# Gated linear attention with an ELU feed-forward on one core: w_in products of 512 columns over pairs of blocks

## The chip, the cores and the metric

The kernel runs on one core of a Trainium2 chip. The metric is the device time of one execution in microseconds (us). Matrix products run on TensorE (PE in the profile, its weight loads PEld), the rest on VectorE (DVE), ScalarE (ACT) and GpSimd (POOL); SyncE (SP) issues nearly all DMAs.

## The reference

```python
def _attn_ref(q, k, v, alpha):            # (B, H, S, D) = (4, 8, 768, 48)
    state = zeros((B, H, D, D))
    for t in range(S):
        state = alpha[:, :, t, :, None] * state + einsum('bhd,bhe->bhde', k[:, :, t], v[:, :, t])
        y[:, :, t] = einsum('bhd,bhde->bhe', q[:, :, t], state)
    return y

def _moe_ref(x, w_in, w_out):             # x: 3072 tokens x 384, w_in 384 x 2048, w_out 2048 x 384
    h = x @ w_in
    g = where(h > 0, h, exp(minimum(h, 0)) - 1)
    return g @ w_out                      # x is y with the heads side by side
```

All tensors are float32. The weights reach the kernel as 64-bit words.

## The kernel before

The attention runs in 24 windows of 128 tokens (`W`; 6 windows per batch element), each cut into two chunks of 64, for all 8 heads at once. The feed-forward runs in 12 blocks of 256 tokens (`BLK`), two windows each, and 8 pairs of 128 hidden columns a block (`NJ`). Each step is a small function, named in an order written out by hand: `START` for the first four blocks, where the weights are unpacked too, and `STEADY`, one round for each later block, with numbers relative to the round. Each engine works through its own instructions in this order.

A window i goes through: L or LA, LB and LV (loads of k, q, alpha and of v), SC (running products of alpha, VectorE), LN and EX (ScalarE), KA, KB, KC (scaled k; VectorE or POOL by the lists KAV, KBV), PC (a check sum), SQ (scaled q), TP and KN or TA, TB, T (k transposed by TensorE and copied by ScalarE, or by VectorE in blocks of 32), S (scores, TensorE), MK (mask), U (new state, TensorE), UA, UB, UC (state of the next window, VectorE), Y (outputs, TensorE), XH and XL (the outputs as two float32r parts, hi by ScalarE and lo by VectorE, in the tile xt), and XD (a DMA that moves the fourth pair of heads into the spare rows of xt). YL, Y3 and XP belong to the first windows.

A weight tile f is loaded by F, unpacked by DA, DB, DC (VectorE), split into two float32r parts by WH (ScalarE) and WL (VectorE, POOL or, after WP, ScalarE). LC, CA and CB read the weights again for a check. X is a filler: two warm-up matmuls of 512 columns without a use.

A step of the feed-forward (b, j) is: A (18 products h = x w_in: two tiles of 128 hidden columns, three tiles of x, three products of hi and lo parts each), RA and RB (ScalarE: relu and exp of -h), RC (VectorE: the ELU), GH and GL (the hi and lo parts of g), and O (12 products, summed over all j in two tiles o of 128 tokens). Z copies the two sums and stores them. V and VP evaluate the checks near the end.

All PSUM tiles (h, o, y, q, u, sc, tp and so on) come from one pool of eight buffers of 128 x 512 (`psa`, tag "pa"); r, gh and gl have three buffers each. Products, with 256 columns in A and 384 in O:

Of the kernel before, what the change touches and what calls it, by code (L numbers as in the profile page):

```python
# [8 lines left out]
F32 = mybir.dt.float32  # L9
# [7 lines left out]
W = 128  # L17
# [5 lines left out]
BLK = 256  # L23
# [6 lines left out]

EARLY = 6
# [17 lines left out]
X.2.2 LA.0 SC.0 LN.0 LB.0 EX.0 KA.0 KB.0 LA.1 SC.1 KC.0 LN.1 LB.1 EX.1 SQ.1 KA.1 KB.1 TP.0 SQ.0 KC.1 S.0 PC.0 MK.0  # L49
F.2 LV.0 KN.0 U.0 UC.0 TP.1 F.0 UA.0 S.1 LV.1 LV.3 KN.1 DA.0 DB.0 U.1 UP.1 UA.1 MK.1 YL.0 Y3.0 X.2.0 PC.1 DC.0 L.2  # L50
UC.1 L.3 YL.1 SC.2 WH.0 LN.2 Y.0 SQ.2 Y3.1 XH.0 EX.2 WH.2 WP.0 F.6 Y.1 SC.3 WL.0 KA.2 KB.2 F.4 KC.2 WP.2 TP.2 XH.1
LN.3 PC.2 XP.1 KN.2 DA.2 XP.0 DB.2 XL.0 XL.1 DC.2 S.2 WL.2 EX.3 WH.6 LV.2 U.2 WH.4 UA.2 KA.3 MK.2 F.1 A.0.0 RA.0.0
# [918 lines left out]
```

## Time and profile before

| | |
|---|---|
| median of 3 runs | 476.09 us (476.07 to 477.59) |
| the profiled execution | 475.45 us, span 473.7 us |
| granted TensorE clock | 0.999 |
| PE, DVE, ACT, POOL busy | 98%, 80%, 64%, 27% of the span |
| h products (L650) | 1728, 128x256 |
| o products (L703) | 1152, 128x384 |

The span goes from the first to the last instruction of the core; the execution's own time holds what lies around it. PE counts matmuls as busy from start to modelled end, and those overlap: what one product costs is read from the distance of starts, or from the pieces of the chain of waits, not from its mean length. In that chain each row is a piece of time: its start, its length, engine, tile and line, and how many instructions.

### The profile page before, as it was taken

To read this page: it belongs to the slowest core of one execution; us is meant where nothing else is said; L and a number is where in the kernel's file an instruction comes from. 1 tells how busy PE (TensorE), PEld (TensorE's weight loads), DVE (VectorE), ACT (ScalarE), POOL (GpSimd) and SP (SyncE) were. 2 spreads that over 40 slices of the span, in tenths; PEclk is the share of its full clock that TensorE was granted. 3 is DMA by queue.
4 is the path that set the end of the run, shared out by engine and by line. 5 is a ranking of instruction groups with operands and counts; after the bars stand their busy time and mean duration, and the time that the engine had idled before them with its cause. 6 is when DMAs were issued, how large, how long until landed. Compare 5 with 4: busy or idle time off the path is not lost.

```text
span 473.7 us, 13243 instructions
## 1 busy us (share of the span) xinstructions
PE 466.6 (98%) x5438; PEld 449.3 (95%) x5438; DVE 381.1 (80%) x770; ACT 303.9 (64%) x696; POOL 126.3 (27%) x111
## 2 busy tenths in 40 slices
PE   7999999999999999999999999999999999999996
PEld 3889999999999999999999999999999999999996
DVE  6999999789888978798898898798898898335331
ACT  4576668664664676867766866867766866655452
POOL 3021432535573512412412421422421520000000
PEclk9999999999999999999999999999999999999999
DMA  8999321621436035425424524424424231210011
GB/s 303 414 413 410 133 71 30 220 65 65 118 108 199 3 82 177 162 69 166 150 70 152 164 72 152 160 75 154 151 85 151 75 94 54 66 43 10 2 36 38
DMA packets 20483, 61.14 MB, mean 129 GB/s; under 512 B 2880, under 2 KB 7872, under 8 KB 20416
## 3 DMA queue, kind: packets, MB, share of 16 engines
q1 hardware_dynamic: 20128, 59.83, 37.9%
q8 instruction: 45, 0.74, 0.7%
q10 hardware_dynamic: 288, 0.39, 0.2%
q14 instruction: 22, 0.18, 0.1%
HBM read 53.53 MB, written 4.72 MB: 123 GB/s over the span
## 4 chain that ended last, share of the span: by engine, by line
PE 96%; ACT 1%; DVE 1%; DMA 1%; POOL 0%; issue 0%; POOLq 0%; DVEq 0%
PE h L650 41%; PE o L703 40%; PE y L452 4%; PE q L368 2%; PE y L447 2%; PE q L323 2%; PE wd L623 1%; PE sc L339 1%; PE tp L274 1%; PE y L492 1%; DMA qka<-in_qka_dram 1%; PE u L386 1%; DVE P L201 1%; PE yl L447 0%; ACT R L215 0%; PE wd L511 0%
## 5 line engine op out<-in xcount | busy, mean ns | idle before, releaser
L650 PE MATMUL h<-xt,w 128*128 128x256 f32 x1728 | 201.1, 276 | 0.2 <-DVE r L669 0.2
L650 PEld LDWEIGHTS h<-xt,w 128*128 128x128 f32 x1728 | 196.8, 192 | 1.5 <-PE tp L274 0.4
L703 PE MATMUL o<-w,gh 128*128 128x384 f32 x768 | 188.2, 327 | 0.0
L703 PEld LDWEIGHTS o<-w,gh 128*128 128x128 f32 x768 | 132.9, 189 | 0.5
L703 PE MATMUL o<-w,gl 128*128 128x384 f32 x384 | 125.3, 326 | 0.0
L658 ACT ACTIVATE r<-h 128x512 f32<-128x512 f32 x96 | 56.3, 597 | 64.3 <-PE h L650 57.2
L284 DVE STREAM_TRANSPOSE kn<-qka 32x128 f32<-32x128 f32 x256 | 77.4, 303 | 4.0
L669 DVE SCALAR_TENSOR_TENSOR h<-r,h 128x512 f32<-128x512 f32 x79 | 53.5, 690 | 28.2 <-ACT r L663 27.8
L703 PEld LDWEIGHTS o<-w,gl 128*128 128x128 f32 x384 | 72.6, 189 | 0.1
L689 DVE TENSOR_TENSOR gl<-h,gh 128x512 fp32r<-128x512 f32 x79 | 53.9, 689 | 18.6 <-ACT gh L675 16.3
L675 ACT CAST gh<-h 128x512 fp32r<-128x512 f32 x79 | 45.9, 581 | 35.6 <-DVE h L669 19.6
L663 ACT ACTIVATE r<-r 128x512 f32<-128x512 f32 x96 | 60.6, 635 | 1.9
L223 POOL TENSOR_TENSOR qka<-qka,R 128x512 f32<-128x512 f32 x18 | 23.2, 1286 | 138.5 <-ACT R L215 86.5
L253 POOL TENSOR_TENSOR st<-qka,P 64x512 f32<-64x512 f32 x30 | 38.0, 1268 | 23.0 <-DVE P L201 13.5
L351 DVE TENSOR_TENSOR st<-q,mask 64x256 f32<-64x256 f32 x72 | 30.3, 421 | 7.8 <-PE q L323 6.4
L228 POOL TENSOR_TENSOR R<-P,R 128x512 f32<-128x512 f32 x20 | 24.4, 1220 | 33.9 <-DVE qka L223 32.5
L210 ACT ACTIVATE R<-P 128x512 f32<-128x512 f32 x24 | 15.2, 631 | 26.9 <-DVE P L201 26.9
L689 POOL TENSOR_TENSOR gl<-r,gh 128x512 fp32r<-128x512 f32 x17 | 24.1, 1426 | 25.9 <-ACT gh L675 17.4
L201 DVE TENSOR_TENSOR_SCAN P<-qka,first 128x516 f32<-128x516 f32 x24 | 29.4, 1224 | 0.9 <-DMA qka<-in_qka_dram 0.8
L606 ACT ACTIVATE ck<-ck,lim 128x384 f32<-128x384 f32 x32 | 23.1, 721 | 0.7
L601 ACT ACTIVATE ck<-ck 128x384 f32<-128x384 f32 x32 | 21.5, 672 | 3.0 <-DMA ck<-in_wgt_dram 3.0
L233 DVE SCALAR_TENSOR_TENSOR qka<-R,qka 128x512 f32<-128x512 f32 x24 | 19.2, 800 | 1.8 <-POOL R L228 1.3
(105 smaller groups left out, 449.0 us busy)
## 6 DMA issues: line engine op xcount, KB each, us to landing
qka<-in_qka_dram SPq DMA_DIRECT2D x22, 770.0 KB, 5.3
raw<-in_wgt_dram SPq DMA_DIRECT2D x16, 768.0 KB, 13.7
ck<-in_wgt_dram SPq DMA_DIRECT2D x32, 384.0 KB, 3.3
vs<-in_vv_dram SPq DMA_DIRECT2D x36, 192.0 KB, 4.2
out_dram<-ot SPq DMA_DIRECT2D x22, 192.0 KB, 2.0
vs<-in_vv_dram SPq DMA_DIRECT2D x6, 384.0 KB, 9.7
xt<-y SPq DMA_DIRECT2D x40, 48.0 KB, 2.2
qka<-in_qka_dram SPq DMA_DIRECT2D x2, 512.0 KB, 5.0
```

Of the source, the lines that this page charges most:

```text
L201: nc.vector.tensor_tensor_scan(out=P.rearrange("p n w -> p (n w)"), data0=t[:, 2 * NP * W:], data1=first.rearrange("p n w -> p (n w)"), in ...
L228: eng(KBV, i).tensor_tensor(out=d["R"], in0=pw(i), in1=d["R"], op=ALU.mult)
L253: eng(SQV, i).tensor_tensor(out=st[r, a], in0=d["q"][r], in1=pw(i)[r], op=ALU.mult)
L284: nc.vector.transpose(out=kn[32 * t:32 * t + 32, :, 32 * g:32 * g + 32], in_=d["kt"][32 * g:32 * g + 32, :, 32 * t:32 * t + 32])
L351: nc.vector.tensor_tensor(out=d["st"][r, a, :, c * C:(c + 1) * C], in0=d["s4"][a][o], in1=mask[o].unsqueeze(1).broadcast_to([64, NP, C]), ...
L650: nc.tensor.matmul(h[:, f, :], lhsT=t[:, wi, ws], rhs=x[:, :, c, xi].rearrange("p a x -> p x a"), start=(f == 0 and k == 0), stop=(k == 8) ...
L658: nc.scalar.activation(out=r, in_=d["h"], func=AF.Relu, scale=-1.0)
L663: nc.scalar.activation(out=d["r"], in_=d["r"], func=AF.Exp, scale=-1.0)
L669: nc.vector.scalar_tensor_tensor(out=d["g"], in0=d["r"], scalar=-1.0, in1=d["h"], op0=ALU.add, op1=ALU.max)
L675: nc.scalar.copy(out=gh, in_=d["g"])
L689: q.tensor_tensor(out=gl, in0=d["g"], in1=d["gh"].bitcast(F32), op=ALU.subtract)
L703: nc.tensor.matmul(o[:, 0:DM], lhsT=gt[:, f, ms], rhs=t[:, wi, f * DM:f * DM + DM].rearrange("p (a x) -> p x a", a=2), start=(j == 0 and f ...
```

## The change

From block 4 on (`PB`) two blocks b and b + 1 are one pair of 512 tokens. The xt tile holds four windows. A step A of a pair computes one tile of 128 hidden columns for all 512 tokens, 9 products of 512 columns; b and j together number the 16 tiles of hidden columns. O takes one tile of hidden columns for four tiles of 128 tokens, so a pair has four sums o, held from its first step O to its last. Z acts once a pair and copies two of its sums by ScalarE and two by VectorE. The stores of the last pair (four, before two of the last block) are issued by ScalarE. START and STEADY, and the lists of who does what, are new. Two more windows go through Y in START. The scratch of dynamic DMAs shrinks to 2048 bytes.

```diff
+PB = 4
-WLV, KAV, KBV, SQV = (1, 7, 9, 10, 11, 14, 15), (0, 1, 2, 3, 4, 7), (0, 1, 2, 6), (1, 2, 3, 5, 7, 10, 11)
-WPE, XPE, GPE, UPE = (0, 2, 4, 6), (0, 1, 2), (), (1,)
+WLV, KAV, KBV, SQV = (1, 3, 9, 11, 13), (0, 1, 2, 3, 5, 6, 11), (0, 2, 3, 4, 5, 11), (0, 1, 5, 7, 9, 10, 11)
+WPE, XPE, GPE, UPE = (0, 2, 4, 6), (0, 1), (), (1,)
...
 STEADY = """
-Y.1 XH.1 Y.0 XL.1 A.-1 RA.-1 A.-3 RA.-3 RB.-3 A.-2 RC.-3 XH.0 XL.0 GH.-3 O.-5 GL.-3 ZV.4 V.0 RB.-1 RC.-1 CA.-12
+U.2 S.2 L.5 A.-3 MK.2.0 UA.2 UB.2 MK.2.1 UC.2 V.0 PC.3 SC.4 CA.-12 CB.-12 O.-5 U.3 S.3 RA.-3 LN.4 L.6 LC.-11 UA.3
...
     def xs(i):
-        blk, half = divmod(i, 2)
-        if blk not in xt:
-            xt[blk] = xpool.tile([128, 2, NC, 2, W], F32R, name="xt", tag="xt")
-        return xt[blk][:, half]
+        pr, k = divmod(i, 4)
+        if pr not in xt:
+            xt[pr] = xpool.tile([128, 4, NC, 2, W], F32R, name="xt", tag="xt")
+        return xt[pr][:, k]
...
     def A(b, j):
-        x = xt[b]
         h = psa.tile([128, 2, BLK], F32, name="h", tag="pa")
         ff[b, j] = dict(h=h)
-        for f in range(2):
+        x = xt[b // 2]
+        for f in range(2 if b < PB else 1):
             k = 0
-            t = wgts[2 * j]
+            r = 2 * j + f if b < PB else b % 2 * NJ + j
+            t = wgts[r // 2 * 2]
             for c in range(NC):
-                ws = slice(f * DM + c * 128, f * DM + c * 128 + 128)
+                ws = slice(r % 2 * DM + c * 128, r % 2 * DM + c * 128 + 128)
                 for wi, xi in ((0, 0), (0, 1), (1, 0)):
-                    nc.tensor.matmul(h[:, f, :], lhsT=t[:, wi, ws], rhs=x[:, :, c, xi].rearrange("p a x -> p x a"),
+                    if b < PB:
+                        o, xv = h[:, f, :], x[:, b % 2 * 2:b % 2 * 2 + 2, :, xi].rearrange("p a c x -> p c x a")[:, c]
+                    else:
+                        o = h.rearrange("p q x -> p (q x)")
+                        xv = x[:, :, c, xi].rearrange("p (q a) x -> p q x a", a=2)
+                    nc.tensor.matmul(o, lhsT=t[:, wi, ws], rhs=xv,
                                      start=(f == 0 and k == 0), stop=(k == 8), skip_group_check=True)
...
     def O(b, j):
-        if j == 0:
-            ops_[b] = [psa.tile([128, 512], F32, name="o", tag="pa") for _ in range(2)]
+        pair = b >= PB
+        key = b // 2 * 2 if pair else b
+        r0 = b % 2 * NJ + j if pair else 2 * j
+        nf = 1 if pair else 2
+        if r0 == 0:
+            ops_[key] = [psa.tile([128, 512], F32, name="o", tag="pa") for _ in range(4 if pair else 2)]
...
     def Z(b):
-        for m in range(2):
-            ot = gpool.tile([128, DM], F32, name="ot", tag="ot")
-            nc.scalar.copy(out=ot, in_=ops_[b][m][:, 0:DM])
+        if b >= PB and b % 2 == 0:
+            return
+        b0 = b // 2 * 2 if b >= PB else b
+        for m, o in enumerate(ops_.pop(b0)):
+            ot = gpool.tile([128, DM], F32, name="ot", tag="ot", bufs=4)
+            if m % 2 and b >= PB:
+                nc.vector.tensor_copy(out=ot, in_=o[:, 0:DM])
+            else:
+                nc.scalar.copy(out=ot, in_=o[:, 0:DM])
 
             q = nc.sync if b < NBLK - 1 else nc.scalar
-            q.dma_start(out=out[b * BLK + m * 128:b * BLK + m * 128 + 128, :], in_=ot)
-        del ops_[b], xt[b]
+            q.dma_start(out=out[b0 * BLK + m * 128:b0 * BLK + m * 128 + 128, :], in_=ot)
```

What stands in a row on TensorE in one round of the steady part. First before: the two Y (L452) stand together ahead of three steps A, and U and S (L368, L323, tile q) of both windows stand together, after one step O. U has half its products (x8) in the last window of a batch element.

```order
L703 MATMUL o<-w_851,gl 128x384
L452 MATMUL y<-st,vs_119 64x64 x16
L452 MATMUL y<-st,vs_118 64x64 x16
L650 MATMUL h<-xt,w_1138 128x256 x18
L650 MATMUL h<-xt,w_861 128x256 x18
```
```order
L703 MATMUL o<-w_851,gl 128x384
L368 MATMUL q<-vs_120,kn 48x48 x16
L323 MATMUL q<-st,qka_133 64x64 x16
L368 MATMUL q<-vs_121,kn 48x48 x8
L323 MATMUL q<-st,qka_134 64x64 x16
L703 MATMUL o<-w_1086,gh 128x384 x2
```

Now (L371 and L326 are U and S, L455 is Y, L659 A, L716 O): U and S of one window, a step A and a step O, U, S and Y, a step O (its first rows shown), and then the other Y ahead of two steps A.

```order
L371 MATMUL q<-vs_118,kn 48x48 x16
L326 MATMUL q<-st,qka_134 64x64 x16
L659 MATMUL h<-xt,w_392 128x512 x9
L716 MATMUL o<-w_714,gh 128x384 x2
L716 MATMUL o<-w_714,gl 128x384
```
```order
L371 MATMUL q<-vs_119,kn 48x48 x16
L326 MATMUL q<-st,qka_132 64x64 x16
L455 MATMUL y<-st,vs_118 64x64 x16
L716 MATMUL o<-w_668,gh 128x384 x2
L716 MATMUL o<-w_668,gl 128x384
```
```order
L716 MATMUL o<-w_668,gl 128x384
L455 MATMUL y<-st,vs_119 64x64 x16
L659 MATMUL h<-xt,w_392 128x512 x18
L716 MATMUL o<-w_668,gh 128x384 x2
L716 MATMUL o<-w_668,gl 128x384
```

Two clumps of small matmuls a round became three, and every step A has half the products, twice as wide.

TensorE's start, first before (L126 warm-ups and fillers, L274 TP, L339 S, L386 U, L412 UP, L447 YL and Y) and then now, where each line number is 3 higher:

```order
L126 MATMUL xf<-first 128x512
L274 MATMUL tp<-ident,qka_132 128x128 x4
L339 MATMUL sc<-st,qka_132 64x64 x16
L386 MATMUL u<-vs_118,kn 64x48 x16
L274 MATMUL tp<-ident,qka_133 128x128 x4
L339 MATMUL sc<-st,qka_133 64x64 x16
L386 MATMUL u<-vs_119,kn 64x48 x16
L412 MATMUL u<-vs_119,minus 128x192 x2
L447 MATMUL yl<-st,vs_118 64x64 x6
```
```order
L129 MATMUL xf<-first 128x512
L277 MATMUL tp<-ident,qka_132 128x128 x4
L342 MATMUL sc<-st,qka_132 64x64 x16
L389 MATMUL u<-vs_118,kn 64x48 x16
L129 LDWEIGHTS first
L129 MATMUL xf<-first 128x512
L129 LDWEIGHTS first
L129 MATMUL xf<-first 128x512
L450 MATMUL yl<-st,vs_118 64x64 x6
L277 MATMUL tp<-ident,qka_133 128x128 x4
L495 MATMUL y<-y_225,sel 64x128 x6
L450 MATMUL y<-st,vs_118 48x64 x18
```

The chain of window 0 goes through to its Y ahead of U and S of window 1, and fillers stand in between.

ScalarE's last instructions, before and now (L658 and L667 RA, L663 and L672 RB, L675 and L684 GH, L712 and L730 the copy in Z, L715 and L733 the store):

```order
L658 ACTIVATE r<-h 128x512
L663 ACTIVATE r<-r 128x512
L675 CAST gh<-h 128x512 x2
L712 COPY ot<-o 128x384
L715 DMA out_dram<-ot 128x384
```
```order
L667 ACTIVATE r<-h 128x512
L672 ACTIVATE r<-r 128x512
L684 CAST gh<-h 128x512 x2
L730 COPY ot<-o 128x384
L733 DMA out_dram<-ot 128x384 x2
```

In both, the copy and the stores come once more behind these rows. There are four stores now, two of them of copies by VectorE.

More of the change, by code (lines that the diff above doesn't have):

```diff
@@ new lines @@
+Y.2 MK.3.1 EX.4 MK.3.0 XH.2 O.-4 RB.-3 Y.3 XH.3 XL.2 A.-2 RC.-3 UB.3 GH.-3 RA.-2 RB.-2 XD.2 CA.-11 XL.3 GL.-3 UC.3
+KA.4 KB.4 SC.5 A.-1 LN.5 EX.5 O.-3 ZV.4 RA.-1 RB.-1 XD.3 KA.5 KB.5 LV.4 RC.-2 GH.-2 CB.-11 A.2 KC.4 T.4.0 T.4.3
+RC.-1 GL.-2 KC.5 A.0 LC.-10 RA.2 GH.-1 GL.-1 LC.-9 T.5.3 T.5.0 RA.0 RB.0 RC.0 T.5.2 CA.-10 CB.-10 RB.2 RC.2 GH.0
+GL.0 O.-2 O.-1 Z.-1 A.1 RA.1 RB.1 RC.1 GH.1 A.3 RA.3 CA.-9 RB.3 T.4.2 GL.1 SQ.5 RC.3 CB.-9 A.4 T.4.1 SQ.4 RA.4 GH.2
+GL.2 RB.4 RC.4 GH.3 GL.3 T.5.1 GH.4 O.0 O.1 O.2 GL.4 LC.-8 VP.0 PC.4 LV.5
@@ L694, in O @@
         gh, gl = d["gh"], d["gl"]
-        if j == 0:
-            ops_[b] = [psa.tile([128, 512], F32, name="o", tag="pa") for _ in range(2)]
-        for m in range(2):
-            o = ops_[b][m]
-            ms = slice(m * 128, m * 128 + 128)
-            for f in range(2):
-                t = wgts[2 * j + 1]
+        pair = b >= PB
[4 more added lines that the diff above has]
+            ops_[key] = [psa.tile([128, 512], F32, name="o", tag="pa") for _ in range(4 if pair else 2)]
+        for m, o in enumerate(ops_[key]):
+            for f in range(nf):
+                r = r0 + f
+                t = wgts[r // 2 * 2 + 1]
+                at = f * BLK + m * 128
                 for k, (gt, wi) in enumerate(((gh, 0), (gh, 1), (gl, 0))):
-                    nc.tensor.matmul(o[:, 0:DM], lhsT=gt[:, f, ms],
-                                     rhs=t[:, wi, f * DM:f * DM + DM].rearrange("p (a x) -> p x a", a=2),
-                                     start=(j == 0 and f == 0 and k == 0),
-                                     stop=(j == NJ - 1 and f == 1 and k == 2))
+                    nc.tensor.matmul(o[:, 0:DM], lhsT=gt.rearrange("p q x -> p (q x)")[:, at:at + 128],
+                                     rhs=t[:, wi, r % 2 * DM:r % 2 * DM + DM].rearrange("p (a x) -> p x a", a=2),
+                                     start=(r == 0 and k == 0), stop=(r == 2 * NJ - 1 and k == 2))
     @tok
     def Z(b):
-        for m in range(2):
-            ot = gpool.tile([128, DM], F32, name="ot", tag="ot")
-            nc.scalar.copy(out=ot, in_=ops_[b][m][:, 0:DM])
+        if b >= PB and b % 2 == 0:
[7 more added lines that the diff above has]
+                nc.scalar.copy(out=ot, in_=o[:, 0:DM])
             q = nc.sync if b < NBLK - 1 else nc.scalar
-            q.dma_start(out=out[b * BLK + m * 128:b * BLK + m * 128 + 128, :], in_=ot)
-        del ops_[b], xt[b]
+            q.dma_start(out=out[b0 * BLK + m * 128:b0 * BLK + m * 128 + 128, :], in_=ot)
     flag = []
@@ L957 @@
     wgt = np.ascontiguousarray(np.stack([wi, wo], axis=1)).view(np.int64).reshape(2 * NJ, 128, 2 * DM)
-    nc = bacc.Bacc("TRN2", target_bir_lowering=False, num_devices=1)
+    nc = bacc.Bacc("TRN2", target_bir_lowering=False, num_devices=1, dynamic_dma_scratch_size=2048)
     arrays, args = {}, []
```

62 lines of the change are left out of this document (29 added, 33 removed).

## The prediction

> **What bounds the kernel now.** I read the page first (busy shares, then the shares of the chain), then TensorE's waits, then the chain of waits over one block of the steady part, then the busy time of the same stretch.
>
> ```profile
> span 473.7 us, 13243 instructions
> PE 466.6 (98%) x5438; PEld 449.3 (95%) x5438; DVE 381.1 (80%) x770; ACT 303.9 (64%) x696; POOL 126.3 (27%) x111
> PE 96%; ACT 1%; DVE 1%; DMA 1%; POOL 0%; issue 0%; POOLq 0%; DVEq 0%
> ```
> TensorE's row of the waits (total, times, longest):
>
> ```profile
> PE wp L126 <- DVE first L120: 2.1, 1, 2.1
> PE tp L274 <- issue: 0.5, 1, 0.5
> PE h L650 <- DVE r L669: 0.2, 1, 0.2
> PE u L386 <- ACT kn L304: 0.2, 1, 0.2
> ```
> These four waits are all that TensorE has in the whole span: three at the start and a single one of 0.2 us later. Between the start and the last w_out product its stream has no hole, so every microsecond that TensorE's own instructions save or cost reaches the end, and other engines count only where they open a hole that isn't there now.
>
> The chain over one block (start, length, what):
>
> ```profile
> 232.26 7.80 PE o L703 x48
> 240.06 2.02 PE y L452 x64
> 242.08 6.22 PE h L650 x54
> 248.30 1.95 PE o L703 x12
> 250.25 0.51 PE q L368 x32
> 250.76 0.48 PE q L323 x32
> 251.24 0.36 PE q L368 x32
> 251.60 0.49 PE q L323 x32
> 252.09 4.10 PE o L703 x24
> 256.18 8.04 PE h L650 x72
> 264.22 1.95 PE o L703 x12
> ```
> And that stretch's busy time, in the order PE, weight loads, DVE, ACT, POOL:
>
> ```profile
> 232.30:268.20 35.90, 35.90 (x434) 35.31 (x433) 31.91 (x76) 24.91 (x61) 9.40 (x8) 1.00 0.42 128
> ```
> This is one block: 8 steps A and 8 steps O, and the attention of two windows in two clumps of small matmuls. A step A (18 products of 256 columns) takes 2.01 us, 111.7 ns a product (8.04 us for 72, four steps). A step O (12 of 384) takes 1.95 us, 162.5 ns each (7.80/48). The clumps also cost at their edges. After one, 54 products take 6.22 us instead of 54 x 111.7 = 6.03, and 24 w_out products 4.10 instead of 3.90: 0.20 us at the exit. At the entry the first U takes 0.51 us, the second, which follows small matmuls, 0.36: 0.15 us. So a clump costs 0.35 us beyond its work. VectorE is busy 31.91 of 35.90 us (89%), so it has 4 us a block to spare, in pieces.
>
> **The change, part by part.**
>
> *Long products.* From block 4 on a step A is 9 products of 512 columns. The trace has 512-column products only in the warm-up and fillers; from the timeline (start, length, count):
>
> ```profile
> 5.56 3.40 PE L126 MATMUL wp<-first 128*128 128x512 bf16 x15
> 8.80 0.38 PE L126 MATMUL xf<-first 128*128 128x512 bf16 x1
> 9.94 0.63 PE L274 MATMUL tp<-ident,qka 128*128 128x128 f32 x4 [0.55 <-issue]
> 11.82 1.27 PE L386 MATMUL u<-vs,kn 128*64 128x48 f32 x32 [0.17 <-ACT kn L304]
> ```
> Fifteen start between 5.56 and 8.80: 216 ns each. In proportion to the 384-column product it would be 216.7. The 256-column product lies 3.4 ns above that proportion (111.7 against 108.3); a long one that did so too would take 220. Bounds 216 and 220; I take 216, the row of this width. A step A is then 9 x 0.216 = 1.944 us, 0.066 less; 64 such steps (blocks 4 to 11) give -4.22 us (with 220: 9 x 0.220 = 1.98, -1.92).
>
> The Trainium skill ("TensorE: Matmul & The Clock Gate", section "Back-to-back issue gap") has a sustained 131 ns for a product of 512 columns in a stream of loads and products. The row above has 216 and 384 columns already take 162.5, so the trace disagrees; by that figure the 576 long products would take 75 us rather than 124.
>
> *More clumps.* Four more pieces of the chain, from the first four blocks (start, length, what):
>
> ```profile
> 17.34 0.54 PE xf L126 x2
> 45.87 0.20 PE y L511
> 81.55 0.44 PE tp L274 x4
> 81.98 1.95 PE o L703 x12
> ```
> The order of the changed kernel splits the attention of two windows into three clumps a block instead of two: U S, then U S Y, then the other Y, with a step O or A between. From the first w_in product to the end I count 25 clumps in the order before and 33 in the order now. Those of tp alone are left out: behind a lone tp the 12 products take their plain 1.95 us (the last two rows). 8 x 0.35 = +2.80 us. Bounds: the entry alone (8 x 0.15 = 1.2) and 0.20 at both edges (3.2). I take the rows' value.
>
> *First four blocks.* One more window is transposed by TensorE (TP, KN) instead of VectorE: +0.44. XP of window 2 goes: -0.20 on TensorE; VectorE does XL instead (0.55 by the row of L533 below) and loses the transposes of the one window, which are more. The filler X has five calls instead of two. Two of the five (four products) stand ahead of the first transposes, where TensorE now waits: the warm-ups end at 8.80 + 4 x 0.216 = 9.66, against 9.94, and the 0.17 us wait for kn ahead of the first U goes too, since SC of window 1 and SQ of window 0 are issued so that S comes first ready: -0.45. The other three calls stand where one stood: 2 x 0.54 = +1.08 (bounds 0, if TensorE would wait there anyway, and 1.08). VectorE's chain to the first weights (DA, DB, DC) keeps its length; on the SP queue the loads of alpha, k, q and v change places, but the same bytes stand ahead of the first weight pair. So I give both nothing; should the start hang on them, the gain of 0.45 goes.
>
> *The end.* The last A steps are now 6 and 7, and O 5, 6, 7 stand behind them; before, a step 6 had O 3 to 5 as cover.
>
> The groups of ScalarE and VectorE in the block shown above (count, busy, mean ns):
>
> ```profile
> L663 ACT ACTIVATE r<-r 128x512 f32<-128x512 f32 x8 | 5.1, 634 | 0.2
> L658 ACT ACTIVATE r<-h 128x512 f32<-128x512 f32 x8 | 4.7, 596 | 4.2 <-PE h L650 4.2
> L675 ACT CAST gh<-h 128x512 fp32r<-128x512 f32 x8 | 4.6, 578 | 2.2 <-DVE h L669 1.1 <-PE o L703 1.0
> L507 ACT ACTIVATE xt<-y 128x384 fp32r<-128x384 f32 x2 | 1.0, 490 | 0.0
> L506 ACT ACTIVATE y<-y 128x128 fp32r<-128x128 f32 x2 | 0.6, 276 | 0.0
> ```
> ```profile
> L669 DVE SCALAR_TENSOR_TENSOR h<-r,h 128x512 f32<-128x512 f32 x8 | 5.5, 690 | 1.5 <-ACT r L663 1.5
> L689 DVE TENSOR_TENSOR gl<-h,gh 128x512 fp32r<-128x512 f32 x8 | 5.4, 688 | 0.4 <-ACT gh L675 0.3
> L533 DVE TENSOR_TENSOR xt<-y,xt 128x384 fp32r<-128x384 f32 x2 | 1.1, 548 | 0.0
> ```
> The transfer of the last rows of xt (page, part 6), the chain's last piece on TensorE, and ScalarE's timeline at the end:
>
> ```profile
> xt<-y SPq DMA_DIRECT2D x40, 48.0 KB, 2.2
> ```
> ```profile
> 459.88 9.77 PE o L703 x60
> ```
> ```profile
> 468.69 0.48 ACT L712 COPY ot<-o 128x384 f32<-128x384 f32 x1 [4.45 <-PE o L703]
> 469.68 0.48 ACT L712 COPY ot<-o 128x384 f32<-128x384 f32 x1 [0.51 <-PE o L703]
> 470.19 0.34 ACTq L715 DMA_DIRECT2D out_dram<-ot  x1
> ```
> With A 6 ending at 0: ScalarE runs RA, RB of step 6 (to 1.25), waits for A 7 (1.94), runs RA, RB of 7 (to 3.2), then GH 6 (3.8); VectorE does RC 7 to 3.9 and only then GL 6, to 4.6. O 5 fills 1.94 to 3.89, and the third product of O 6 (4.2) waits for GL 6: +0.4 us, 0.5 with hand-overs. GL 7 is done at 5.3, ahead of O 7. Before, the last five O run without a hole (9.77 = 60 x 0.163). Then four sums are stored instead of two, by ScalarE's queue: copy, store, the store of a VectorE copy, copy, store, store. The third and fourth of them begin when the last sum is ready and need 0.48 + 2 x 0.34 = 1.16, where one copy and one store (0.82) stood: +0.4 with the wait for VectorE's copies. Together +0.9 (0.3, the stores alone, to 1.0).
>
> *At no cost, with the cover named.* Z comes once a pair; its two VectorE copies (near 0.55, the row of L533, which also reads 128x384 of such a buffer) stand where O 7 has ended and three steps A (5.8 us) follow before the next pair's first O. The first A of a pair needs the second Y of its own block's round, by way of XH (0.28 and 0.49, with a read of the accumulator between), XL (0.55) and XD on the SP queue: 1.6 us with hand-overs, and 2.2 for the transfer: two steps A and one O, 5.8 us, stand between. If VectorE were 2 us late there, that cover would be gone. POOL keeps KA, KB and SQ of the later windows, 9.40 of 35.90 us. Larger xt tiles and the smaller DMA scratch move no instruction. The w_out products keep their number and width.
>
> Sum: -4.22 + 2.80 + 0.44 - 0.20 - 0.45 + 1.08 + 0.9 = +0.35 us. The profiled execution took 475.45 us (span 473.7 and 1.75 around it); it would be 475.8. The median of the three runs, 476.09, stands 0.64 above that execution, so I add the sum to the median: 476.4. About 0.3%, 1.4 us, is what a measurement of this kernel can tell from no change.
>
> **The rivals.**
>
> *Faster.* The edges cost less than counted or fillers only fill. With half of the exit price hidden by the 216 ns that a long product gives the next load, 14 of the clumps now (two a block, seven blocks) lose 0.10 each of their exit, -1.4, and fillers at 0 give another -1.08: 476.4 - 2.5 = 473.9. For it: a long product leaves twice the time for whatever comes late there. Against it: the exit costs 0.20 before 256 columns and 0.20 before 384, so width has hidden nothing so far. Chance 0.26.
>
> *Slower, by accumulator buffers.* Four of the eight are held by the pair's sums through both blocks, two before. The second A behind the last Y can take only the buffer which that Y leaves: the 1.6 us of XH and XL, against one step A of 1.94 and the exit 0.2 as cover. That leaves 0.5 us. It decides from the point where VectorE reaches this subtraction 0.5 us late; with 1 us late it is 7 x 0.5 = 3.5 us: 479.9; from 0.7 us late on the result is slower. For it: VectorE's 89%. Against it: the mask products, the state updates and RC that stand ahead of it there end, added up by their rows, about when ScalarE is done. Chance 0.15.
>
> *Slower, by the width.* If a long product takes 220 ns, the gain is 1.92 instead of 4.22: +2.3, 478.7. Chance 0.08.
>
> *Overlapping products.* If consecutive long products needed no more than the 162.5 ns of a 384-column one, 576 x 53.5 ns = 30.8 us would go: 445.6. The 216 ns of the warm-up speak against it. The skill's 131 ns, named above, is a rule of this kind. Chance 0.01.
>
> **How the numbers follow.** The likeliest case, all terms as summed, has 0.50 and 476.4. Faster by over 0.3% (below 474.66): 0.27, the first and last rival. Slower (above 477.52): 0.23, the two in between. Within: 0.50. The range goes from 474.0, the first rival nearly whole, to 479.0, the width rival whole and the nearer half of the buffer rival.
>
> **What would show it.** The chain's 9-product steps at 1.94 us, blocks of 35.7 us instead of 35.9, three clumps a block with 0.20 at each exit; the first U near 11.4 us; TensorE's waits still short, with one of about 0.5 on gl near the end and the end of the span 0.4 us later behind the last product. The forecast is wrong if TensorE waits for VectorE's xt or h once a block, if long products pace other than 216, or if the first steps A come more than 1 us early or late against the work that stands ahead of them.

## The result, and the profile after

| | median, us | ratio to before, with its 95% interval |
|---|---|---|
| before | 476.09 | |
| changed | 480.52 (479.34 to 481.60, five runs) | 1.0096, 1.0075 to 1.0116 |

The change made the kernel slower by about 1%, some 4.4 us between the medians; the forecast was 476.4 and a range of 474.0 to 479.0. The profiled execution took 481.55 us. Its page has these lines (span; busy time and share of the span by engine; shares of the chain that ended last):

```profile
span 479.7 us, 12075 instructions
...
PE 468.8 (98%) x4868; PEld 431.9 (90%) x4871; DVE 383.1 (80%) x766; ACT 303.8 (63%) x688; POOL 124.3 (26%) x108
...
PE 88%; DVE 5%; ACT 2%; DMA 2%; issue 1%; POOL 0%; SPq 0%; DVEq 0%; ACTq 0%; POOLq 0%
```

TensorE is as full as before (98%), but less of the chain runs through it: 88% instead of 96%. The pieces of VectorE and of the transfers stand ahead of a single wait, at 102 us: in the traces that don't have it (e_tail and e_load below, for two) the chain is 96% TensorE again. TensorE's waits behind its start (total, times, longest):

```profile
...
PE h L659 <- DVE r L678: 1.2, 1, 1.2
PE o L716 <- DVE gl L698: 0.3, 1, 0.3
PE o L716 <- POOL gl L698: 0.2, 1, 0.2
```

Behind the start there are these three, all new: 1.2 us at 102 us, one for POOL's GL at 170 us, and the one for GL 6 (the lo part of g of step 6) at the end. None of them returns from block to block, so the steady part is paced by TensorE's own work. Its chain over one block (start, length, what), and that stretch's busy time (PE, weight loads, DVE, ACT, POOL):

```profile
210.16 0.51 PE q L371 x32
210.66 0.48 PE q L326 x32
211.15 2.14 PE h L659 x9
213.28 1.95 PE o L716 x12
215.24 0.51 PE q L371 x32
215.74 0.48 PE q L326 x32
216.22 1.08 PE y L455 x32
217.30 2.15 PE o L716 x12
219.45 1.08 PE y L455 x32
220.53 4.08 PE h L659 x18
224.61 1.95 PE o L716 x12
226.56 3.88 PE h L659 x18
230.45 3.90 PE o L716 x24
234.35 5.83 PE h L659 x27
240.18 5.85 PE o L716 x36
```
```profile
210.09:245.96 35.87, 35.87 (x362) 32.99 (x361) 32.10 (x75) 26.43 (x63) 10.19 (x8) 1.00 0.38 116
```

A plain long step A takes 1.94 us (3.88 for two, 5.83 for three), as forecast, and a step O 1.95. Yet the block takes 35.87 us, where 35.90 stood before and 35.7 was forecast. The small products explain it: two U of 0.51 and two Y of 1.08, where before one U took 0.51, the other 0.36, and both Y together 2.02; and three exits (2.14 for a step of 1.94, 2.15 for 1.95, 4.08 for 3.88) instead of two.

All runs below are divided at the same places. "First U" is the start of the first product U. "Seam" is the end of step O 3.2, the last TensorE piece of the order of the first four blocks, taken as the start of the product behind it, so that a wait just there counts with the time to the seam (e_old3 and best2). The numbers are worked out from the starts of TensorE's products in each trace: from the first U to the seam, from there to the end of the last product, and from there to the end of the span. Each ratio is against executions of the kernel before taken beside that run, with medians of 475.8 to 477.3 us, so ratios compare the rows better than medians do.

| run | median | ratio, interval | first U | to the seam | to the last product | end |
|---|---|---|---|---|---|---|
| before | 476.09 | | 11.82 | 156.41 | 301.40 | 4.11 |
| changed | 480.52 | 1.0096, 1.0075 to 1.0116 | 12.22 | 161.73 | 299.08 | 6.71 |
| e_nopair | 482.15 | 1.0117, 1.0085 to 1.0148 | 11.26 | 161.77 | 303.31 | 4.26 |
| e_clump | 478.41 | 1.0041, 1.0019 to 1.0063 | 12.11 | 156.38 | 304.08 | 4.10 |
| e_two | 483.26 | 1.0126, 1.0099 to 1.0154 | 11.74 | 162.62 | 301.50 | 6.62 |
| e_edge | 482.28 | 1.0134, 1.0111 to 1.0157 | 11.70 | 160.62 | 300.71 | 7.00 |
| e_fill | 481.04 | 1.0111, 1.0088 to 1.0133 | 12.29 | 161.19 | 299.00 | 6.52 |
| e_load | 480.15 | 1.0088, 1.0068 to 1.0107 | 11.89 | 160.24 | 299.28 | 6.54 |
| e_oldstart | 482.51 | 1.0121, 1.0093 to 1.0150 | 12.25 | 155.45 | 307.20 | 6.74 |
| e_old2 | 483.47 | 1.0138, 1.0108 to 1.0168 | 11.58 | 158.63 | 304.97 | 6.94 |
| e_old3 | 486.32 | 1.0215, 1.0192 to 1.0237 | 11.76 | 164.72 | 300.90 | 6.69 |
| e_old4 | 482.05 | 1.0122, 1.0090 to 1.0153 | 12.13 | 158.44 | 302.85 | 6.37 |
| e_tail | 480.16 | 1.0079, 1.0050 to 1.0107 | 12.64 | 160.24 | 299.00 | 6.30 |
| e_tail2 | 481.08 | 1.0099, 1.0073 to 1.0125 | 11.84 | 160.25 | 299.00 | 7.07 |
| e_tail3 | 479.87 | 1.0089, 1.0064 to 1.0114 | 11.74 | 160.25 | 299.28 | 6.24 |
| e_half | 481.42 | 1.0104, 1.0074 to 1.0133 | 11.67 | 161.71 | 299.63 | 6.02 |
| e_mmajor | 479.88 | 1.0066, 1.0044 to 1.0088 | 12.90 | 160.36 | 299.26 | 5.45 |
| best | 488.50 | 1.0246, 1.0220 to 1.0272 | 11.86 | 159.44 | 307.89 | 6.37 |
| best2 | 485.71 | 1.0195, 1.0174 to 1.0216 | 11.52 | 164.81 | 302.15 | 6.22 |
| best3 | 481.01 | 1.0098, 1.0071 to 1.0125 | 12.46 | 158.45 | 302.98 | 5.35 |

### The profile page after: what moved, and what is told of

It is laid out like the page before. It is cut to its first block, busy times and chain, and to the rows that moved or that the text cites. A ratio compares the mean times of both kernels' runs of the same rounds, so it can differ in the third digit from the quotient of the medians.

```text
span 479.7 us, 12075 instructions
## 1 busy us (share of the span) xinstructions
PE 468.8 (98%) x4868; PEld 431.9 (90%) x4871; DVE 383.1 (80%) x766; ACT 303.8 (63%) x688; POOL 124.3 (26%) x108
## 4 chain that ended last, share of the span: by engine, by line
PE 88%; DVE 5%; ACT 2%; DMA 2%; issue 1%; POOL 0%; SPq 0%; DVEq 0%; ACTq 0%; POOLq 0%
PE h L659 36%; PE o L716 35%; PE y L455 4%; DMA qka<-in_qka_dram 2%; PE q L371 2%; PE q L326 2%; PE wp L129 2%; PE wd L626 1%; PE sc L342 1%; PE y L450 1%; PE tp L277 1%; PE y L495 1%; ACT r L672 1%; DVE h L678 1%; DVE r L678 1%
## 5 line engine op out<-in xcount | busy, mean ns | idle before, releaser
L659 PE MATMUL h<-xt,w 128*128 128x256 f32 (+1 forms) x1152 | 199.8, 329 | 1.2 <-DVE r L678 1.2
L716 PE MATMUL o<-w,gh 128*128 128x384 f32 x768 | 188.6, 328 | 0.0
L659 PEld LDWEIGHTS h<-xt,w 128*128 128x128 f32 x1152 | 173.2, 190 | 16.7 <-DVE r L678 1.3
L716 PEld LDWEIGHTS o<-w,gh 128*128 128x128 f32 x768 | 134.7, 189 | 2.5 <-ACT gh L684 0.2
L716 PE MATMUL o<-w,gl 128*128 128x384 f32 x384 | 125.4, 327 | 0.5 <-DVE gl L698 0.3
L667 ACT ACTIVATE r<-h 128x512 f32<-128x512 f32 x96 | 57.3, 597 | 68.4 <-PE h L659 66.0
L678 DVE SCALAR_TENSOR_TENSOR h<-r,h 128x512 f32<-128x512 f32 x80 | 55.1, 690 | 40.0 <-ACT r L672 39.0
L287 DVE STREAM_TRANSPOSE kn<-qka 32x128 f32<-32x128 f32 x240 | 72.6, 303 | 4.0
L716 PEld LDWEIGHTS o<-w,gl 128*128 128x128 f32 x384 | 72.6, 189 | 1.1 <-DVE gl L698 0.6
L684 ACT CAST gh<-h 128x512 fp32r<-128x512 f32 x80 | 47.0, 587 | 25.2 <-DVE h L678 15.4
L672 ACT ACTIVATE r<-r 128x512 f32<-128x512 f32 x96 | 60.6, 634 | 1.6
L256 POOL TENSOR_TENSOR st<-qka,P 64x512 f32<-64x512 f32 x28 | 36.0, 1287 | 1.3
L204 DVE TENSOR_TENSOR_SCAN P<-qka,first 128x516 f32<-128x516 f32 x24 | 31.3, 1309 | 2.0 <-DMA qka<-in_qka_dram 1.1
L609 ACT ACTIVATE ck<-ck,lim 128x384 f32<-128x384 f32 x32 | 25.8, 806 | 0.5
L231 POOL TENSOR_TENSOR R<-P,R 128x512 f32<-128x512 f32 x18 | 22.4, 1242 | 12.2 <-DVE qka L226 11.1
L455 PE MATMUL y<-st,vs 128*64 128x64 f32 x576 | 20.3, 225 | 0.0
```

Source lines behind the costliest of these rows:

```text
L204: nc.vector.tensor_tensor_scan(out=P.rearrange("p n w -> p (n w)"), data0=t[:, 2 * NP * W:], data1=first.rearrange("p n w -> p (n w)"), in ...
L256: eng(SQV, i).tensor_tensor(out=st[r, a], in0=d["q"][r], in1=pw(i)[r], op=ALU.mult)
L287: nc.vector.transpose(out=kn[32 * t:32 * t + 32, :, 32 * g:32 * g + 32], in_=d["kt"][32 * g:32 * g + 32, :, 32 * t:32 * t + 32])
L455: nc.tensor.matmul(out[64 * a:64 * a + m], lhsT=lhs(i, c, a)[:, n * D:n * D + m], rhs=d["st"][:, a, n, c * C:(c + 1) * C], start=start, st ...
L659: nc.tensor.matmul(o, lhsT=t[:, wi, ws], rhs=xv, start=(f == 0 and k == 0), stop=(k == 8), skip_group_check=True)
L667: nc.scalar.activation(out=r, in_=d["h"], func=AF.Relu, scale=-1.0)
```

## The experiments

The theory that the expectations call "the ledger" was drawn up from the first trace of the changed kernel: the pairs gain what was forecast, and it is paid back by a dearer third clump, by the new order of the first four blocks, and by VectorE's late branch at the end. The first stood. The new order does cost time up to the seam, but none was had back by leaving it, and the late branch is not what makes the end late.

**e_nopair: the changed order without pairs** (`PB = 12` instead of `4`).

> The changed kernel with PB = 12: its order throughout, but no pairs, so every step A has 18 products of 256 columns, and two stores at the end as before. Theory (the ledger): the pairs' gain of 4.3 us goes, the late end of 2.2 us and the wait for GL 6 (0.4) go too, the rest of the loss stays: 480.5 + 4.3 - 2.6 = 482.2 (481.5 to 483.0), blocks of 36.4 us. Rival: the pairs cost something themselves (four accumulators held, XT of two blocks); then the time comes out nearer 480, with blocks of 36.0 or less.

Measured 482.15 us. Behind the seam TensorE takes 303.31 us without pairs and 299.08 with them: the pairs gain 4.23 us on TensorE, 4.22 was forecast. (The wait for GL 6 is in both, so it belongs to the new order and not to the pairs.) The end is 4.26 instead of 6.71, so what is left of the gain in the whole time is less than 2 us. The new order without pairs is 1.2% slower than the old one. That the pairs cost something themselves in the steady part is refuted.

**e_clump: the kernel before, its two Y apart.**

```
- Y.1 XH.1 Y.0 XL.1 A.-1 RA.-1 A.-3
+ Y.1 XH.1 XL.1 A.-1 RA.-1 Y.0 A.-3
```


> The kernel before with one edit in its steady order: the two products Y of a block, which stood together, get a step A between them, so that each of eight blocks has three clumps of small products instead of two; nothing else moves. Theory (the ledger): a clump costs 0.49 us: 8 x 0.49 = 3.9, so 480.0 (479.3 to 480.6). The prediction's price, 0.35: 478.9. If a clump cost nothing and only the order of the windows' work counted: 476.1.

```profile
204.69 1.08 PE y L452 x32
205.77 2.21 PE h L650 x18
207.97 1.08 PE y L452 x32
209.06 4.21 PE h L650 x36
```

That is the new clump in the chain: 1.08 twice where 2.02 stood (+0.14), and a second exit, 2.21 for a step of 2.01 (+0.20). Behind the seam TensorE takes 304.08 - 301.40 = 2.68 us more, 0.335 for each of eight clumps. So the prediction's price of 0.35 was right for one clump more, and the ledger's 0.49 is not the price of a clump. The ratio says 2 us (0.9 to 3.0).

**e_edge: which neighbours a clump has.** O.-5 goes ahead of A.-3, and Y.2 ahead of U.3 and S.3.

```
- U.2 S.2 L.5 A.-3 MK.2.0 ... O.-5 U.3 S.3 RA.-3 ... UA.3 Y.2 MK.3.1
+ U.2 S.2 L.5 O.-5 A.-3 MK.2.0 ... Y.2 U.3 S.3 RA.-3 ... UA.3 MK.3.1
```


> The changed kernel with two pieces of the steady order exchanged: step O.-5 ahead of A.-3, so that the second clump of small products follows a long step A, and in that clump the products Y ahead of U and S instead of behind them; still three clumps a block. The transitions in the traces so far say: a small product behind a w_out product starts 0.093 us late and behind a long w_in product not at all; a Y behind S starts 0.12 us late and a U behind Y not at all. Theory (price by kind of transition): 0.10 + 0.12 a block, blocks of 35.65 us instead of 35.87, seven of them: 480.5 - 1.5 = 479.0. Rival (a clump costs what it costs, whatever stands beside it): blocks stay at 35.87 and the time at 480.5. If Y 3 comes too early for VectorE, TensorE waits for it once a block and the time rises.

```profile
213.57 1.08 PE y L455 x32
214.65 0.51 PE q L371 x32
215.16 0.48 PE q L326 x32
215.63 2.15 PE o L716 x12
217.78 1.13 PE y L455 x32
...
218.91 2.22 PE h L659 x9
...
221.18 2.18 PE h L659 x9
```

The expectation was wrong. Y behind a long step still takes 1.08, and now the U behind Y takes 0.51 where I expected 0.36. So each beginning of a row of U and S, or of Y, costs its 0.14 to 0.15 in these rows, whichever of the kinds here stands ahead of it; only a U S behind a U S, or a Y behind a Y, is spared. In addition the Y at 217.78 and the two steps A behind it come late (4.45 for both where 4.08 stood), and behind the seam it takes 1.6 us more. What holds those two steps was not followed.

With this the block can be added up. Before it had two beginnings (Y, U) and two exits, now four beginnings (U, U, Y, Y) and three exits: 0.15 + 0.14 + 0.20 = 0.49. The prediction charged one beginning and one exit, 0.35.

**e_two: the two clumps put together again.**

```
- U.2 S.2 L.5 A.-3 MK.2.0 ... O.-5 U.3 S.3 RA.-3 ... UA.3 Y.2 MK.3.1 EX.4 MK.3.0 XH.2 O.-4 RB.-3 Y.3
+ U.2 S.2 L.5 MK.2.0 ... U.3 S.3 O.-5 A.-3 RA.-3 ... UA.3 O.-4 MK.3.1 EX.4 MK.3.0 Y.2 XH.2 RB.-3 Y.3
```


> The changed kernel with the small products of the steady part put into two clumps a block instead of three: U S U S of both windows in one, both Y in the other, as they stood before; the steps A and O that stood between follow behind. Theory (the ledger of the steady block): a block loses two edges of a clump and the switch from S to Y inside one, 0.48 us, so blocks of 35.4 us and 480.5 - 7 x 0.48 = 477.1 (476.5 to 477.8). By the prediction's price, 0.35 a clump: 478.1. Rival: the three clumps are what four accumulators held through a pair force; with all four small results of two windows beside them no accumulator is free, TensorE waits 0.5 us or more a block for VectorE there, and the time stays at 480.5 or rises.

TensorE's wait that is new, and the chain at one of its four places:

```profile
PE h L659 <- DVE xt L536: 3.5, 4, 0.9
```
```profile
217.87 1.10 PE y L455 x32
...
219.37 0.48 ACT xt L510 x2
...
219.87 0.29 DVE y L532
220.16 0.47 DVE xt L536
...
220.77 1.32 PE h L659 x5
```

The rival held. Blocks without the wait take 35.56 us, 0.30 less than in the changed kernel, and the others 36.5 and more. The step A behind the last Y has no free accumulator and stands until that Y has been read by XH and XL. This is the prediction's rival of the accumulator buffers, but it is not in the changed kernel: there a step O between the two Y covers it. What it shows is why the clumps stand apart: with four accumulators held, putting them together costs more than the edges that it saves.

**e_fill: without three of the five filler calls** (X.2.1, X.2.12, X.2.11 taken out).

> The changed kernel without the three calls of the filler product X that stand behind the first U (X.2.1, X.2.12, X.2.11). Theory (the prediction's term): they stand on TensorE's path, six products of 512 columns, and their removal brings up to 1.08 us: from the first U to the first step A 21.6 us instead of 22.7, time 479.4. Rival: TensorE would wait there anyway for VectorE and ScalarE; then 22.7 stays and the time is 480.5.

From the first U to the first step A it takes 22.16 us instead of 22.69: 0.53 less, half of what was expected. TensorE waits 0.8 us for ScalarE at a YL there instead. The time did not fall.

**e_load: L.7 ahead of F.13 and F.15.**

```
- O.0.3 F.13 RC.1.4 ... F.15 L.7 GL.1.2
+ O.0.3 L.7 F.13 RC.1.4 ... F.15 GL.1.2
```


> The changed kernel with the load of q, k and alpha of window 7 (L.7) issued ahead of the weight loads F.13 and F.15 instead of behind them. Theory: in the changed kernel that load stands some 33 us behind a weight load that waits for its buffer, lands at 94.5 to 95.5 us, about when VectorE wants it, and where it lands late TensorE loses 1.4 us at 102 us. Issued early it is there in every execution: no wait of TensorE near 102, 160.2 us from the first U to the seam instead of 161.7, and the time is 1.0 lower than the changed kernel's median or more: 479.0 to 479.7. Rival: the late piece there is VectorE's own backlog, not the load; then the wait stays and the time is 480.5.

The changed kernel's wait on SyncE's queue, and the chain at its wait of TensorE at 102 us:

```profile
SPq L563 <- DVE w L637: 32.6, 1, 32.6
```
```profile
85.70 9.79 DMA qka<-in_qka_dram
...
95.51 1.92 DVE P L204
...
99.31 1.72 DVE qka L236
...
102.85 0.60 DVE r L678
...
103.50 0.60 PE h L659 x3
```

POOL's R in the changed kernel, and the scan (P) in e_tail, which has no wait at 102 us:

```profile
95.15 1.18 POOL L231 TENSOR_TENSOR R<-P,R 128x512 f32<-128x512 f32 x1 [3.53 <-DVE qka L226]
```
```profile
95.35 1.23 DVE L204 TENSOR_TENSOR_SCAN P<-qka,first 128x516 f32<-128x516 f32 x1
```

The weight load F.13 blocks SyncE's queue for 32.6 us, and L.7 behind it lands when VectorE wants it. In e_load it is issued at 55.42 us instead of 85.70, and TensorE has no wait there. But the wait is in the traces of the changed kernel, e_nopair, e_two, e_fill and e_half, and not in those of e_tail, e_tail2, e_tail3, e_edge and e_mmajor, which have the same order there: in these the load landed in time by itself. So it is a matter of a microsecond, in five of ten traces of that order, worth 1.5 us up to the seam where it strikes (161.73 against 160.25 in e_tail2). How late the load is does not matter: VectorE waits 0.2 to 0.9 us for it in the five traces, and TensorE behind it 1.1 to 1.2 in each of them. What they share is that POOL's R starts ahead of the scan; the scan then takes 1.49 to 2.22 us instead of 1.23 and ends 1.09 us behind POOL's R in all five. In the other five, and in e_load, the scan comes first and POOL's R takes 1.98 to 2.04 instead of 1.18. So a load that misses by a little lets POOL go first. That e_load's median (480.15) lies 0.4 below the changed kernel's agrees with that and proves little.

**The old order of the first four blocks.** e_oldstart takes it, with its lists of engines, and puts `Y.9 XH.9 Y.8 XL.9 XH.8 XL.8 XD.9 XD.8` behind its end. e_old2 puts Y.8 behind A.3.4 and Y.9 behind A.3.2 instead. e_old3 also takes TP.10 and KN.10 on TensorE and ScalarE for TA.10 and TB.10 on VectorE. e_old4 moves KN.10 ahead of CA.3.

> The changed kernel with the order of the first four blocks as it was before (its lists of engines too), and behind it the two products Y of windows 8 and 9 that the pairs need there; pairs, the order of the steady part and the last stores stay as changed. Theory (the ledger): the new order of the first four blocks costs 3.3 us (fillers, later first products, two waits of TensorE between 100 and 170 us), so 480.5 - 3.3 = 477.2 (476.3 to 478.0), with the first U at 11.8 and no wait of TensorE over 0.3 us until the last steps. Rival: the loss is in the pairs and their steady part; then 479.5 or more.

> The changed kernel with the order of the first four blocks as before, and the two products Y of windows 8 and 9 put between steps A of the fourth block (behind A 3.4 and A 3.2) instead of in one lump at the seam. Theory (the ledger by stretches): 155.5 us from the first U to the seam as the old order takes without the hoisted Y pieces, 2.5 for the two Y, 299.0 for the rest, 6.7 at the end: 477.2 (476.5 to 478.0), with no wait over 0.5 us at the seam. Rival: what the pairs need at the seam (two Y early, a buffer XT of four windows) costs the old order as much as the new one loses; then 479.5 or more.

> The kernel with the old order of the first four blocks, pairs, and Y 8 and Y 9 between steps A (as two runs before), and window 10 transposed by TensorE (TP.10, KN.10) instead of VectorE (TA.10, TB.10). Theory: VectorE's transposes of window 10 were what TensorE waited for at the seam (2.4 us, and then a granted clock of 0.5 for 6 us); without them no wait over 0.5 us at the seam, 159.2 us from the first U to the seam, 299.1 behind it, 480.5 - 1.5 = 479.0 (478.2 to 479.8): the new order of the first four blocks costs about 1 to 1.5 us by itself. Rival: VectorE is late at the seam for its other work too (XL, XD of two windows more); the wait stays at 1 us or more and the time is 481 or more.

> The kernel with the old order of the first four blocks, pairs, Y 8 and Y 9 between steps A, window 10 transposed by TensorE, and its copy KN.10 ahead of ScalarE's check of a weight half (CA.3) instead of behind it. Theory: without the wait at the seam 158.6 us from the first U to the seam (164.7 less the 6.2 of that wait) against 160.25 in the new order without its wait at 102 us, 299.1 behind it: 478.6 (477.7 to 479.6); the new order costs 1 to 1.5 us by itself, and the granted clock stays at 1 at the seam. Rival: at the seam ScalarE or VectorE is late with the next piece, and a wait of 1 us or more comes in its place: 480 or more, and then the old order is no better with pairs than the new one.

All four expected the old order to be 1.5 to 3.3 us better, and none was (ratios 1.0121 to 1.0215 against 1.0096; only e_old3's interval lies clear of the changed kernel's). Up to the seam the old order is indeed cheaper: 158.44 us in e_old4 against 160.25 in the new order without its wait at 102 us. Behind the seam it loses 3.75 us (302.85 against 299.1). The wait there, in e_oldstart for ScalarE's copies and VectorE, in e_old2 and e_old4 for VectorE's SQ:

```profile
PE q L325 <- DVE st L255: 2.6, 2, 2.4
```
```profile
PE q L325 <- DVE st L255: 1.6, 2, 1.3
```

The first row is e_old2, the second e_old4. In e_old4 the granted clock also fell behind that wait, to 0.76 over 2.8 us and 0.74 over the next 4.0, which takes another 1.7 us: together most of the 3.75. In best3, which has the same order, the same wait left the clock at 1.00, but two more waits of 0.6 us followed, and it took 302.98. (e_old3 waited 6.2 us for KN.10, which its own edit had put behind CA.3, and CA.3 waits for a transfer; e_old4 mends that.) The two Y that the pairs need at the seam bring VectorE two XL more there, and it was full. So the rival holds as far as these runs go: no time was had back by leaving the new order of the first four blocks. In the profiled executions it is the cheaper one for the pairs (459.24 us from the first U to the last product in e_tail, 461.29 in e_old4).

**The end.** e_tail lets ScalarE do all four last copies. e_tail2 in addition stores two sums at a time. e_tail3 issues the four stores from SyncE. e_half leaves out the first two stores. e_mmajor gives each sum the products of O 6 and O 7 before the next sum starts.

> The changed kernel, but the last pair's four sums are all copied by ScalarE, none by VectorE. Theory (the ledger): VectorE's last copy holds its branch at the end back by some 9 us, and its code fetches then fall on the last stores. With VectorE free early, the last store lands about 2 us earlier: the span ends 4.3 to 4.8 us behind the last product instead of 6.65, and the time is 478.5 (477.9 to 479.0) instead of 480.5. Rival: the four stores themselves are the cost. Then four copies of 0.48 and four stores of 0.34 on one queue (3.3 us of work from 1.5 us ahead of the last product on) end later than now, and the time stays at 480.5 or rises to 481.

> The changed kernel, but the last pair's four sums are copied by ScalarE into two buffers of two sums each, and each buffer leaves in one store: two stores instead of four, VectorE free early. Theory: the end behind the last product is made of the time of the last store's issue and of code fetches that fall on it; the last issue comes 0.95 us behind the last product, as now, but lands 2 to 2.7 us later instead of 4.1: end 4.5 to 5.2 us behind the last product instead of 6.7, time 478.3 to 479.0. Rival: stores of twice the size, or ScalarE's own branch, take as long; then 6.2 us or more and 480 or more.

> The changed kernel with the last pair's four stores issued by SyncE's queue instead of ScalarE's; the four copies stay as they are, two on ScalarE, two on VectorE. Theory: the time at the end goes with when the last store is issued and with the code fetch of 16 KB that starts 1.6 us behind the last product on one of the transfer engines; without issues between its copies ScalarE is done at 0.6 us, the last store is issued some 0.3 us earlier than now, but the fetch still falls on it: 6.3 us behind the last product instead of 6.7, 480.1. Rival: the fetch follows ScalarE's own stream and moves with it; then the stores are through ahead of it or behind it, and the end is 4.5 us or less: 478.3.

> The changed kernel without the stores of the first two of the last pair's four sums (their rows of the output are left out; the copies stay). Theory (bytes in flight): a code fetch of 16 KB comes on one transfer engine 1.6 to 2.6 us behind the last product; with two stores fewer that engine is through with its packets before or soon after, and the end is 4.3 to 4.8 us behind the last product instead of 6.2 to 7.1; time about 478.5. Rival: it is not the amount but the fetch's time alone; with the last stores issued 0.6 and 1.0 us behind the last product as now, the end stays at 6 us or more and the time at 480 or more.

> The changed kernel with the last two steps O (6 and 7) sum by sum: each sum gets the products of both steps before the next one starts, so the four sums finish 0.97 us apart instead of 0.49. Theory (bytes in flight when the fetch comes): copies and stores of the first three sums are over by then, the end is 4.3 to 5.2 us behind the last product, a wait for GL 7 of 0.3 us comes in before: 478.9 (478.2 to 479.6). Rival: the last store alone meets the fetch and takes as long as four did; then 6 us or more stay, and the time is 480.5 or a little above.

The end of the changed kernel on ScalarE, VectorE's last copy, and the last transfers (GB/s in 40 slices from 470 to 480 us; stores, KB each, median us from issue to landing):

```profile
472.11 0.91 ACTq L733 DMA_DIRECT2D out_dram<-ot  x2
473.12 0.48 ACT L730 COPY ot<-o 128x384 f32<-128x384 f32 x1 [1.03 <-PE o L716]
473.63 0.82 ACTq L733 DMA_DIRECT2D out_dram<-ot  x2
```
```profile
473.07 0.56 DVE L728 COPY ot<-o 128x384 f32<-128x384 f32 x1 [0.42 <-PE o L716]
```
```profile
GB/s 0 0 0 0 0 0 66 0 0 0 0 6 332 375 350 369 142 43 385 332 338 371 68 6 57 18 12 12 25 31 6 33 0 0 0 0 0 0 0 0
...
out_dram<-ot ACTq DMA_DIRECT2D x4, 192.0 KB, 3.0
```

The stores run at up to 385 GB/s until 475.5 us, and then a trickle of 6 to 68 goes on for 2.5 us. Its packets come one behind the other, some of them at 150 to 220 ns instead of 65, as from a single one of the sixteen transfer engines that is late with its share; code fetches of 16 KB and 8 KB are under way at that time. That they run on the same engine is inferred from this and not shown. In the kernel before and in e_nopair the same row reads:

```profile
out_dram<-ot ACTq DMA_DIRECT2D x2, 192.0 KB, 1.9
```
```profile
out_dram<-ot ACTq DMA_DIRECT2D x2, 192.0 KB, 2.3
```

VectorE's late branch is not the reason: in e_tail and e_tail2 it branches 3.2 us ahead of the last product, and the end is still 6.30 and 7.07. The queue is not (e_tail3, 6.24), nor the amount of data: e_half has two stores, issued 0.06 and 0.63 us behind the last product, and ends at 6.02, while the kernel before, whose last store goes out at 0.56, ends at 4.11. What differs is when the 16 KB fetch begins: 2.56 and 2.60 us behind the last product in the two kernels without pairs whose rows stand above, when their stores were through (last packet at 2.08 and 2.14), but 1.6 to 2.1 in e_half, e_tail, e_tail2, e_tail3, e_mmajor and the changed kernel. That agrees with the fetch meeting the stores. In e_load and e_old3 it began only at 2.54 and 2.67, but their last stores were issued at 1.21 and 1.33; with the 1.5 us that the last store of the kernel before took from its issue to its last packet (0.56 to 2.08) they were under way then too, and the end was 6.54 and 6.69. No run moved the fetch alone, so that it holds the stores back is argued and not shown, and what sets its time was not found. e_mmajor, whose first three stores are issued before the last product, has the shortest end of these, 5.45 us, and the smallest ratio, 1.0066. Of the five expectations only e_tail3's held.

**Put together.** best: old order as in e_old2, clumps as in e_two, stores as in e_tail2. best2: e_old3 and e_mmajor. best3: e_old4 and e_mmajor.

> The three together: old order of the first four blocks with the two Y placed as in the run before, two clumps a block in the steady part, two stores at the end. Theory: the pairs' gain of 4.3 us is then not given back: 477.2 - 3.4 - 2.0 = 471.8 (470.5 to 473.5), faster than the kernel before (476.1). Rival (accumulators short): two clumps cost waits of TensorE in every block, and the time comes out at 475 or more.

> The two runs before together: old order with window 10 on TensorE, pairs, and the last two steps O sum by sum. If both theories hold, 479.0 - 1.6 = 477.4 (476.6 to 478.4), still not faster than the kernel before (476.1); if only one holds, 479 to 480.

> The run e_old4 with the last two steps O sum by sum, and nothing else. If the end comes out at 5.5 us behind the last product: 1.2 less than e_old4, so 477.4 (476.4 to 478.6), not faster than the kernel before (476.1). If the fetch at the end meets the last store all the same, the end stays at 6.2 and the time at 478.2.

None came near the kernel before, and all three expectations failed. best has the waits of e_two and of e_old2 (488.5); best2 has the 6.3 us wait of e_old3 (485.7). best3 shows an end of 5.35 us again, so what e_mmajor saves there repeats, but not the gain forecast for the whole: 481.01. No version with pairs that was tried beats the kernel before.

## Why the prediction was wrong

The forecast was 476.4 and 480.52 was measured, 4.1 us more. The largest part of that is one term: the stores at the end, put at 0.4, cost 2.6. The clumps and the first four blocks cost some 1 us more than their terms, the earlier first U (0.45) did not come, and a wait of TensorE behind a moved load, put at nothing, makes 0.7 in the mean. Point by point, by its own steps:

- *Long products, -4.22: right.* 4.23 us between e_nopair and the changed kernel, and 1.94 us for nine products (216 ns each). The rivals of width and of overlapping products are dead with it.
- *More clumps, +2.80: mis-sized.* One clump more costs 0.335 (e_clump), as the rows said. But the step counted clumps and left out that Y now stands behind S in one of them, where it pays a beginning of its own. The block's loss is 0.49, so +1.0 over seven blocks. The tell-tale was in the rows quoted: 0.51 and 0.36 for the same U.
- *First four blocks, fillers +1.08: at most half of it.* All three calls behind the first U, one more than the term counts, bring 0.53 when they go (e_fill).
- *First U 0.45 earlier: wrong, in the mean nothing.* The start hangs on how many of the 25 warm-up products take 427 ns instead of 216, 6 to 14 in these traces, whatever the kernel. With 6 the changed order starts U at 11.26 (e_nopair), near the forecast 11.37; with 14 at 12.90. The old order passes less of it on: 11.52 and 11.82 with 6, 12.46 with 14. Over all traces both start at 11.9 to 12.0 in the mean. The step set a calculation against one execution, whose warm-up was the shortest kind, 6.
- *"The same bytes stand ahead", loads at nothing: wrong.* The prediction looked only as far as the first weight pair. L.7 behind a blocked weight load costs 1.5 us in half of the traces of that order, and POOL's GL at 170 us another 0.2 in all traces of that order (the row of waits).
- *The end, +0.9: the wait right, the stores mis-sized.* The wait for GL 6 is there (0.581 us between two products that else stand 0.163 apart, so 0.42). The stores were taken to cost 0.4 and cost 2.6 (6.71 - 4.11), because the price was that of their issue, not of their landing. Why they land so late is argued above and open.
- *Rival "by accumulator buffers", 479.9:* its time came near the result by luck, its mechanism is not there. It appears when the clumps are put together (e_two).

As a sum of what was measured, from the first U to the last product and against 457.81 before: -4.2 (pairs), +3.4 (seven blocks of 0.49), +1.8 (new order of the first four blocks, e_tail against e_old4), +0.5 (window 10 on TensorE), +0.3 (its two Y apart), +0.4 (GL 6), and -0.96, since in the order before six products of Y stood between those of O 3.1 and the old order without them takes 155.45 instead of 156.41. That is +1.2; e_tail, which does not have the wait at 102 us, measures +1.4 (459.24). With 2.6 at the end and 1.5 in every second execution it makes some 4.7 in the mean; measured are 4.4 between the medians. What stays open is whether the code fetch is what holds the last stores back and what starts it, and what parts of the 1.8 are other than fillers and POOL's wait.

## What to carry to other kernels

Price a move of small products by the beginnings of each kind of product, not by the number of groups, and look in the trace for the same instruction at two places with two lengths. When a change makes buffers live longer (here four accumulators instead of two), the order around them may have to be loosened to cover it, as it was here, and that loosening is the change's price: work it out before the gain. A price taken from the issue of the last stores is not the price of their landing.

## What the runs showed of the hardware

- After a wait of 2.4 us TensorE ran at half its clock. e_old2 (each row: stretch, length, busy time by engine, then the granted clock, the transfer share and GB/s):

```profile
170.00:173.20 3.20, 0.82 (x33) 0.48 (x31) 3.06 (x10) 1.75 (x5) 1.27 (x1) 0.94 0.19 36
173.20:176.00 2.80, 2.55 (x37) 2.25 (x38) 2.67 (x8) 1.18 (x4) 0.00 (x0) 0.50 0.30 109
176.00:180.00 4.00, 4.00 (x20) 4.00 (x20) 3.75 (x12) 1.45 (x5) 0.00 (x0) 0.54 0.78 237
```

  The clock stays at 0.50 to 0.54 for nearly 7 us, which takes 2.80 x 0.50 + 4.00 x 0.46 = 3.2 us of full clock: more than the wait itself. The wait of 1.2 us at 102 us in the changed kernel left the clock at 1.00. The Trainium skill ("TensorE: Matmul & The Clock Gate", "What's actually happening") puts the drop behind an idle window of about 3.4 us; here a wait of 2.4 was enough. In e_old4 even one of 1.35 us (with 0.25 more behind it) was followed by a clock of 0.51 from 174.6 to 178.0 us (the 0.76 and 0.74 above are the same fall, over other stretches), while the same wait left it at 1.00 in best3, so the length of the wait alone does not decide it.
- The number of warm-up products at half speed varies between executions: 6 in the trace of before, 14 in those of e_mmajor and best3. The same section of the Trainium skill has 6, 11 or 14 for one kernel; the traces agree, with 6 to 14.
- Each beginning of a row of small products (U and S, or Y) cost 0.14 to 0.15 us, behind long products (U 0.51 against 0.36) and behind small ones of the other kind (Y 1.08 each against 2.02 for two), and each exit to long ones 0.20 (2.14 for a step of 1.94). The Trainium skill ("TensorEngine Tiling (Array Packing)", "Key Properties") has TensorE drained when the tiling mode changes, without a price; the traces agree that there is a cost; whether it is that drain, no run here tells.
